# Attention and an expert layer in one kernel: the softmax of later batches moved to VectorE, and the order of work in the first two chunks changed

## The chip, the cores and the metric

The kernel runs on one core of one Trainium2 chip. The metric is device time in microseconds (us) of one execution. Each time given is the median of several runs, and one execution is also recorded by the hardware profiler. The core's engines are TensorE (PE, matrix products; PEld is its weight load), VectorE (DVE), ScalarE (ACT), GpSimd (POOL) and SyncE (SP, which issues the DMAs here). Each works through a queue of its own in order.

## The reference

Two stages, all in float32: attention with a window over 8 batches of 8 heads, 576 positions and 64 dimensions a head, then a two-layer block with an ELU.

```python
scores = q @ k.T / sqrt(64)              # per batch and head
rel = pos[:, None] - pos[None, :]
mask = (rel >= 0) & (rel < 32)                           # heads 0 to 3
mask = (rel >= 0) & (rel < 128) & (rel % 4 == 0)         # heads 4 to 7
attn = softmax(where(mask, scores, -1e9))
x = (attn @ v), heads side by side       # 4608 x 512
h = x @ w_in                             # 512 x 2048
g = where(h > 0, h, exp(min(h, 0)) - 1)
out = g @ w_out                          # 2048 x 512
```

The weights arrive as float64 bit patterns and are converted to float32 on the chip.

## The kernel before, in words

**Chunks.** The 4608 rows of x are taken in 9 chunks (c) of 512. For each chunk the 2048 hidden units are taken in 16 groups (f) of 128. Gemm1 of an f multiplies a 128-column slice of w_in with the chunk's x into a PSUM tile h; `elu` turns it into g; gemm2 adds g times w_out's rows into four PSUM banks (`o_ps`). Gemm2 of f is put two f behind gemm1 (LAG), so PE's order is gemm1(f), any attention work placed at f, gemm2(f - 2). PE keeps the order in which the program states its products. All products have one line in the profile, L82, and are told apart by their tiles: h is gemm1, o_ps gemm2, a_ps the attention's scores and outputs (in later chunks, tile h receives most of the attention's outputs too, from pt and vt).

**Two kinds of product.** A product is either one float32 matmul (recorded as two) or three float32r matmuls: each operand is split into a high part and a remainder, and high x high, high x low and low x high are added. For x the parts are xh and xl (`split_x`, L302 on ACT and L303 on DVE); for weights wh and wl (`split_w`, L131 on ACT and L132 on DVE); for g they are gh and gl (L340 on ACT, L341 on DVE). In chunk 0 both gemms use float32 for f < 12 (F0), since splits aren't ready; the float64 conversion (`magnitude` L102 on ACT, `convert` L110 to L115 on DVE) runs one weight pair after another through chunk 0. From f = 12 on all is float32r. The raw weights live in tiles r, their float32 form in tiles a, and the splits are written into whichever of these have come free.

**Elu.** For f < 12 of chunk 0: exp (L330) and a relu (L332) on ACT, one step on DVE (L334). Otherwise ACT first copies h from PSUM to SBUF (L328; one buffer), then exp (L330) on ACT, two steps on DVE (L336, L337), then gh on ACT and gl on DVE. In chunks 1 to 6 h has one PSUM bank (h0), as the other (h1) receives attention outputs; otherwise it has two.

**Attention.** The heads are handled in 4 pairs per batch. For a pair, 36 small products per head give the scores for 6 query blocks of 96 (windows of 64 keys each); DVE adds the mask (L253), takes the maximum (L254) and scales it (L255); ACT computes 12 exponentials with the sum accumulated (L259); sums are inverted (L181, L182) and multiplied in (L183, on DVE for batch 1, on POOL for later ones); six transposes on DVE (L265) write pt; PE multiplies with v, and ACT copies the outputs into x32 (L173, L176). Batch 0 is done before chunk 0 with other code (`first_attention`). Batch 1 is done during chunk 0 by the generator `batch_attention`, whose 8 steps are spread over f. Batches 2 to 7 are done during chunks 1 to 6, batch c + 1 during chunk c, in `piece`s: at a piece PE computes the outputs of the last pair and the scores of the next. The places of pieces are the f in `when`:

```python
when = () if c == 0 or c >= B - 1 else (0, 4, 7, 10, 12) if c == 1 else (2, 5, 9, 12)
```

So in chunk 1 the first piece only starts a softmax (at f = 0), and the last one starts batch 3.

**Order.** The program is laid out by a scheduler with a timing model: it fills each engine's queue by the order of statements and by when it believes operands are ready. `tc.issue_after(ins)` places the instructions of a block behind `ins` in that instruction's engine queue, with no wait of its own.

Of the kernel before, what the change touches and what calls it, by code (L numbers as in the profile page):

```python
# [46 lines left out]
def body(ctx: ExitStack, tc: tile.TileContext, q, k, v, masks, w_in, w_out, out):  # L47
# [69 lines left out]
    def split_w(k):  # L117

        if k >= K0:
            both = wst.tile([P, 2, 2, DM], F32R, name=f"r{k - K0}")  # L120
            h, l = both[:, 0, :, :], both[:, 1, :, :]
        else:
            l = wst.tile([P, 2, DM], F32R, name=f"a{k - 1}")
            slot = NF - K0 + k // 2
            if slot < NR:
                if k % 2 == 0:
                    split_w.room = wst.tile([P, 2, 2, DM], F32R, name=f"r{slot}")
                h = split_w.room[:, k % 2, :, :]
            else:
                h = wst.tile([P, 2, DM], F32R, name=f"a{K0 + k - 2 * (NR - NF + K0)}")  # L130
        nc.scalar.copy(out=h, in_=full2[k])  # L131
        nc.vector.tensor_tensor(out=l, in0=full2[k], in1=h.bitcast(F32), op=ALU.subtract)  # L132
        for t in range(2):
            wh[need[2 * k + t]], wl[need[2 * k + t]] = h[:, t, :], l[:, t, :]
# [108 lines left out]
    def probabilities(b, hp, loaded, s_ps):  # L243
# [11 lines left out]
        nc.vector.tensor_scalar(out=nmx, in0=nmx, scalar1=-0.125, scalar2=None, op0=ALU.mult)  # L255
        for u in range(2 * NU):
            if u == NU:
                yield
            nc.scalar.activation(out=sm[:, u, :], in_=sm[:, u, :], func=AF.Exp, bias=nmx[:, u:u + 1], scale=0.125, accum_out=sums[:, u:u + 1])  # L259
        normalise(nc.vector if b < 2 else nc.gpsimd, sm, sums, lambda ins: ins)  # L260
        tr = transposed()
        for c in range(GU):
            for r in range(2):
# [1 line left out]
                nc.vector.transpose(out=tr[ks, :, cs], in_=sm[cs, :, rs])  # L265
# [58 lines left out]
    def elu(h_ps, first):  # L324
        e = fp.tile([P, TC], F32, name="e", bufs=3)
        if not first:
            h = fp.tile([P, TC], F32, name="h", bufs=1)
            freed.append(nc.scalar.copy(out=h, in_=h_ps).ins)  # L328
# [1 line left out]
        nc.scalar.activation(out=e, in_=h_ps, func=AF.Exp)  # L330
# [6 lines left out]
        hidden.append(nc.vector.scalar_tensor_tensor(out=e, in0=h_ps, scalar=0.0, in1=e, op0=ALU.max, op1=ALU.add).ins)  # L337
# [20 lines left out]
    def batch_attention(b):  # L358

        x32[b] = xp.tile([P, NPAIR, S], F32, name="x32", bufs=2)  # L360

        old = None
        for hp in range(NPAIR):
            *_, new = probabilities(b, hp, loaded_pairs.pop((b, hp)), banks())
# [167 lines left out]
```

## Time and profile before

| what | value |
|---|---|
| median of 3 runs | 916.41 us (916.23 to 916.5) |
| profiled execution, its own time | 916.74 us |
| its span | 915.0 us |
| mean clock granted to PE | 0.991 |
| PE busy | 891.9 us (97%) |
| DVE busy | 553.6 us (61%) |
| ACT busy | 462.1 us (51%) |
| POOL busy | 46.3 us (5%) |
| DMA | 59.40 MB, mean 65 GB/s |

The span is from the first to the last recorded work. Chunk 0 takes roughly 30 to 140 us of it, chunk 1 140 to 249, and each of chunks 2 to 6 some 97 us. The share of an engine is an average over stages with different limits. In the timeline's rows, a bracket tells how long the engine stood idle just before, and what ended it. Matmuls overlap: rows can be longer than the distance to the next row's start, and it is this distance that counts.

### The profile page before, as it was taken

What the parts mean: (1) busy time and instruction counts of PE and PEld (TensorE: products, weight loads), DVE (VectorE), ACT (ScalarE), POOL (GpSimd) and SP (SyncE); (2) the same over time, 40 slices, a digit from 0 to 9 for tenths busy, and PEclk for the clock granted to TensorE, in tenths of its full rate; (3) what the DMA queues carried; (4) which work ended last, traced back from release to release, by engine and by line L of the source; (5) the groups of instructions that cost most, each with busy time, mean ns of one, the idle gap of its engine ahead of it and who ended that gap; (6) DMA issues with size and microseconds to landing.
All of it is one profiled execution on the core that took longest, in us unless ns stands there. A gap on an engine that the chain in (4) does not pass through costs nothing.

```text
span 915.0 us, 16120 instructions
## 1 busy us (share of the span) xinstructions
PE 891.9 (97%) x6536; PEld 698.0 (76%) x6536; DVE 553.6 (61%) x926; ACT 462.1 (51%) x1317; POOL 46.3 (5%) x36
## 2 busy tenths in 40 slices
PE   5999999998999999999999999999999999999998
PEld 4544458876888888888788888888888888888886
DVE  5999989676647565566565565656475433343332
ACT  4754595554555446545554555555545443344333
POOL 2000000100001000001000000000000000000000
PEclk8999999998999999999999999999999999999999
DMA  9963111111121112111121202111200010001001
GB/s 350 403 234 119 44 36 67 51 45 51 40 90 44 46 44 91 45 45 45 47 79 33 67 1 91 45 54 36 91 19 1 1 47 1 0 1 47 1 1 46
DMA packets 23803, 59.40 MB, mean 65 GB/s; under 512 B 2640, under 2 KB 2736, under 8 KB 23728
## 3 DMA queue, kind: packets, MB, share of 16 engines
q1 hardware_dynamic: 23728, 58.37, 18.7%
q8 instruction: 51, 0.84, 0.4%
q14 instruction: 24, 0.20, 0.1%
HBM read 48.92 MB, written 9.44 MB: 64 GB/s over the span
## 4 chain that ended last, share of the span: by engine, by line
PE 72%; DVE 14%; ACT 7%; DMA 4%; issue 3%; SPq 0%; ACTq 0%; DVEq 0%
PE h L82 35%; PE o_ps L82 33%; PE a_ps L82 3%; DVE pt L265 3%; DMA r<-w_out 2%; DVE e L337 2%; ACT sm L259 2%; DVE a L115 1%; DVE a L113 1%; ACT xh L302 1%; DVE a L132 1%; ACT r L131 1%; ACT h L328 1%; DMA r<-w_in 1%; DVE a L110 1%
## 5 line engine op out<-in xcount | busy, mean ns | idle before, releaser
L82 PE MATMUL o_ps<-a,gh 128*128 128x512 f32 x576 | 205.5, 426 | 0.0
L82 PE MATMUL o_ps<-r,gh 128*128 128x512 f32 x576 | 194.3, 396 | 0.3 <-ACT gh L340 0.3
L340 ACT CAST gh<-e 128x512 fp32r<-128x512 f32 x132 | 82.1, 622 | 217.7 <-DVE e L337 217.7
L82 PE MATMUL h<-xh,r 128*128 128x512 f32 x512 | 183.8, 393 | 0.8 <-ACT h L328 0.5
L82 PE MATMUL h<-xh,a 128*128 128x512 f32 x480 | 147.8, 389 | 0.0
L336 DVE TENSOR_SCALAR e<-e 128x512 f32<-128x512 f32 x132 | 56.2, 426 | 150.7 <-ACT e L330 148.3
L82 PE MATMUL o_ps<-r,gl 128*128 128x512 f32 x368 | 144.4, 392 | 1.5 <-DVE gl L341 1.5
L82 PE MATMUL h<-xl,r 128*128 128x512 f32 x368 | 143.3, 389 | 0.0
L328 ACT COPY h<-h 128x512 f32<-128x512 f32 x132 | 77.0, 583 | 128.3 <-PE h L82 128.3
L82 PEld LDWEIGHTS o_ps<-a,gh 128*128 128x128 f32 x576 | 107.3, 188 | 39.0 <-issue 19.6
L259 ACT ACTIVATE sm<-sm,nmx 96x64 f32<-96x64 f32 x336 | 112.4, 337 | 43.0 <-DVE nmx L255 43.0
L341 DVE TENSOR_TENSOR gl<-e,gh 128x512 fp32r<-128x512 f32 x132 | 91.3, 692 | 66.8 <-ACT gh L340 55.8
L82 PEld LDWEIGHTS o_ps<-r,gh 128*128 128x128 f32 x576 | 108.6, 190 | 24.3 <-ACT gh L340 0.5
L337 DVE SCALAR_TENSOR_TENSOR e<-h,e 128x512 f32<-128x512 f32 x132 | 119.0, 902 | 4.5
L82 PEld LDWEIGHTS h<-xh,r 128*128 128x128 f32 x512 | 96.3, 188 | 23.8 <-ACT h L328 3.2
L82 PEld LDWEIGHTS h<-xh,a 128*128 128x128 f32 x480 | 90.1, 188 | 18.8
L330 ACT ACTIVATE e<-h 128x512 f32<-128x512 f32 x144 | 90.4, 628 | 20.9 <-PE h L82 18.6
L265 DVE STREAM_TRANSPOSE pt<-sm 32x384 f32<-32x384 f32 x168 | 95.4, 568 | 1.9
L82 PEld LDWEIGHTS o_ps<-r,gl 128*128 128x128 f32 x368 | 69.6, 189 | 16.6 <-DVE gl L341 1.9
L82 PEld LDWEIGHTS h<-xl,r 128*128 128x128 f32 x368 | 69.2, 188 | 14.9 <-issue 0.7
L183 POOL TENSOR_TENSOR sm<-sm,sums 96x768 f32<-96x768 f32 x24 | 40.3, 1680 | 644.8 <-ACT e L330 644.8
L181 DVE TENSOR_SCALAR sums<-sums 96x12 f32<-96x12 f32 x32 | 6.0, 189 | 108.9 <-ACT sm L259 108.7
(92 smaller groups left out, 824.2 us busy)
## 6 DMA issues: line engine op xcount, KB each, us to landing
vt<-v SPq DMA_DIRECT2D x30, 384.0 KB, 3.4
kt<-k SPq DMA_DIRECT2D x30, 304.0 KB, 4.7
qt<-q SPq DMA_DIRECT2D x30, 288.0 KB, 4.3
r<-w_in SPq DMA_DIRECT2D x16, 512.0 KB, 8.1
r<-w_out SPq DMA_DIRECT2D x16, 512.0 KB, 8.3
out<-o SPq DMA_DIRECT2D x32, 256.0 KB, 2.2
out<-xl SPq DMA_DIRECT2D x4, 256.0 KB, 2.1
r<-v SPq DMA_DIRECT2D x2, 384.0 KB, 8.6
```

The lines of the kernel that those rows point to most:

```text
L82: inorder(nc.tensor.matmul(*args, **kw))
L110: keep(nc.vector.tensor_scalar(out=a, in0=a, scalar1=TINY, scalar2=None, op0=ALU.max))
L113: keep(nc.vector.scalar_tensor_tensor(out=au, in0=hi, scalar=0xC0000000, in1=au, op0=ALU.bitwise_and, op1=ALU.bitwise_or))
L183: return keep(eng.tensor_tensor(out=sm, in0=sm, in1=sums.unsqueeze(2).broadcast_to([QB, 2 * NU, 2 * G]), op=ALU.mult))
L259: nc.scalar.activation(out=sm[:, u, :], in_=sm[:, u, :], func=AF.Exp, bias=nmx[:, u:u + 1], scale=0.125, accum_out=sums[:, u:u + 1])
L265: nc.vector.transpose(out=tr[ks, :, cs], in_=sm[cs, :, rs])
L328: freed.append(nc.scalar.copy(out=h, in_=h_ps).ins)
L330: nc.scalar.activation(out=e, in_=h_ps, func=AF.Exp)
L336: nc.vector.tensor_scalar(out=e, in0=e, scalar1=1.0, scalar2=-1.0, op0=ALU.min, op1=ALU.add)
L337: hidden.append(nc.vector.scalar_tensor_tensor(out=e, in0=h_ps, scalar=0.0, in1=e, op0=ALU.max, op1=ALU.add).ins)
L340: nc.scalar.copy(out=gh, in_=e)
L341: nc.vector.tensor_tensor(out=gl, in0=e, in1=gh.bitcast(F32), op=ALU.subtract)
```

## The change

- **Float32r in chunk 0.** F0 = 12 becomes two numbers: gemm1 uses float32r from f = 9 (F1), gemm2 from f = 14 (F2). `split_w` takes parts of a weight pair (only the w_in half for pairs 8 to 14 in chunk 0), and `space` hands out room for the parts. `split_x(0)` comes at f = 6 instead of 8. In chunk 1 the remaining parts are split: pairs 0 to 7 whole, 8 to 14 by half.
- **Elu.** Through chunk 0, and in chunks 7 and 8, h isn't copied to SBUF. All of chunk 0 uses ACT's relu.
- **Softmax of batches 2 to 7.** DVE subtracts the maximum, ACT computes one exponential over the pair's whole tile (96 x 768), DVE sums it, and DVE (not POOL) multiplies. Batch 1 keeps the old form, on DVE throughout. `probabilities` is divided into `exponentials` (E) and `probabilities` (X), and nothing is held back to the next f in a piece.
- **Places.** Batch 1's steps are written out, one entry per f: scores and exponentials (E) at f = 1, 3, 7, 11; X at 2, 4, 8, 12; outputs (O) at 5, 9, 14, 15, where before the outputs were at 5, 9, 13, 14. The pieces of chunk 1 move from (0, 4, 7, 10, 12) to (0, 3, 6, 9, 12).
- **Order.** Several `issue_after` anchors move with it.

The diff, cut to its core:

```diff
-F0 = 12
-K0 = F0 - 1
+F1 = 9
+F2 = 14
...
+    spaces = [[f"r{i}", 4] for i in range(NR)] + [["a-1", 2]]
+    taken = {}
+    def space(n):
+        s = next(s for s in spaces if s[1] >= n)
+        if s[0] not in taken:
+            taken[s[0]] = wst.tile([P, s[1], DM], F32R, name=s[0]), s[1]
+        room, all_of = taken[s[0]]
+        o = all_of - s[1]
+        s[1] -= n
+        return room[:, o:o + n, :]
+    def split_w(k, t0, t1):
+        h, l = space(t1 - t0), space(t1 - t0)
+        w = full2[k][:, t0:t1, :]
+        nc.scalar.copy(out=h, in_=w)
+        nc.vector.tensor_tensor(out=l, in0=w, in1=h.bitcast(F32), op=ALU.subtract)
+        for t in range(t0, t1):
+            wh[need[2 * k + t]], wl[need[2 * k + t]] = h[:, t - t0, :], l[:, t - t0, :]
+        if all(wh[need[2 * k + t]] is not None for t in range(2)):
+            spaces.append([f"a{k}", 2])
...
-        nc.vector.tensor_scalar(out=nmx, in0=nmx, scalar1=-0.125, scalar2=None, op0=ALU.mult)
-        for u in range(2 * NU):
-            if u == NU:
-                yield
-            nc.scalar.activation(out=sm[:, u, :], in_=sm[:, u, :], func=AF.Exp, bias=nmx[:, u:u + 1], scale=0.125, accum_out=sums[:, u:u + 1])
-        normalise(nc.vector if b < 2 else nc.gpsimd, sm, sums, lambda ins: ins)
+        if b == 1:
+            nc.vector.tensor_scalar(out=nmx, in0=nmx, scalar1=-0.125, scalar2=None, op0=ALU.mult)
+            for u in range(2 * NU):
+                nc.scalar.activation(out=sm[:, u, :], in_=sm[:, u, :], func=AF.Exp, bias=nmx[:, u:u + 1], scale=0.125, accum_out=sums[:, u:u + 1])
+        else:
+            nc.vector.tensor_tensor(out=sm, in0=sm, in1=nmx.unsqueeze(2).broadcast_to([QB, 2 * NU, 2 * G]), op=ALU.subtract)
+            nc.scalar.activation(out=sm, in_=sm, func=AF.Exp, scale=0.125)
+            nc.vector.tensor_reduce(out=sums, in_=sm, op=ALU.add, axis=mybir.AxisListType.X)
+        return b, hp, vt, sm, sums
+    def probabilities(b, hp, vt, sm, sums):
+        normalise(nc.vector, sm, sums, lambda ins: ins)
         tr = transposed()
         for c in range(GU):
             for r in range(2):
                 ks, cs, rs = slice((c + r) * G, (c + r + 1) * G), slice(c * G, (c + 1) * G), slice(r * G, (r + 1) * G)
-                nc.vector.transpose(out=tr[ks, :, cs], in_=sm[cs, :, rs])
+                last_transpose[b] = nc.vector.transpose(out=tr[ks, :, cs], in_=sm[cs, :, rs]).ins
+        return b, hp, vt, tr
...
-        if c == 0 and f < F0:
+        if c == 0 and f < F1:
...
-    def elu(h_ps, first):
+    def elu(h_ps, c, f):
         e = fp.tile([P, TC], F32, name="e", bufs=3)
-        if not first:
+        if 0 < c < B - 1:
             h = fp.tile([P, TC], F32, name="h", bufs=1)
-            freed.append(nc.scalar.copy(out=h, in_=h_ps).ins)
+            nc.scalar.copy(out=h, in_=h_ps)
             h_ps = h
         nc.scalar.activation(out=e, in_=h_ps, func=AF.Exp)
-        if first:
+        if c == 0:
             below.append(nc.scalar.activation(out=e, in_=e, func=AF.Relu, scale=-1.0, bias=1.0).ins)
-            g = fp.tile([P, TC], F32, name="gh", bufs=3)
-            hidden.append(nc.vector.scalar_tensor_tensor(out=g, in0=h_ps, scalar=0.0, in1=e, op0=ALU.max, op1=ALU.subtract).ins)
-            return g, None
-        nc.vector.tensor_scalar(out=e, in0=e, scalar1=1.0, scalar2=-1.0, op0=ALU.min, op1=ALU.add)
-        hidden.append(nc.vector.scalar_tensor_tensor(out=e, in0=h_ps, scalar=0.0, in1=e, op0=ALU.max, op1=ALU.add).ins)
+            if f < F2:
+                g = fp.tile([P, TC], F32, name="gh", bufs=3)
+                hidden.append(nc.vector.scalar_tensor_tensor(out=g, in0=h_ps, scalar=0.0, in1=e, op0=ALU.max, op1=ALU.subtract).ins)
+                return g, None
+            hidden.append(nc.vector.scalar_tensor_tensor(out=e, in0=h_ps, scalar=0.0, in1=e, op0=ALU.max, op1=ALU.subtract).ins)
+        else:
+            nc.vector.tensor_scalar(out=e, in0=e, scalar1=1.0, scalar2=-1.0, op0=ALU.min, op1=ALU.add)
+            nc.vector.scalar_tensor_tensor(out=e, in0=h_ps, scalar=0.0, in1=e, op0=ALU.max, op1=ALU.add)
...
+    def second_attention():
+        x32[1] = xp.tile([P, NPAIR, S], F32, name="x32", bufs=2)
+        state = [None] * NPAIR
+        for step in " E0 X0 E1 X1 O0  E2 X2 O1  E3 X3  O2 O3".split(" "):
+            if step:
+                what, hp = step[0], int(step[1])
+                if what == "E":
+                    state[hp] = exponentials(1, hp, loaded.pop((1, hp)), banks())
+                    load_next(1, hp)
+                elif what == "X":
+                    state[hp] = probabilities(*state[hp])
+                else:
+                    b, _, vt, tr = state[hp]
+                    outputs(b, hp, [(a, i * NA, (i + 1) * NA) for i, a in enumerate(banks())], vt, tr)
             yield
-            if old is not None:
-                outputs(*old[:2], [(a, i * NA, (i + 1) * NA) for i, a in enumerate(banks())], *old[2:])
-                yield
-            old = new
-        outputs(*old[:2], [(a, i * NA, (i + 1) * NA) for i, a in enumerate(banks())], *old[2:])
...
-            with tc.issue_after(hidden[F0 - 4]), tc.issue_after(below[F0 - 4]):
-                split_x(c)
+            with tc.issue_after(hidden[-4]), tc.issue_after(below[-4]):
+                last_x = split_x(c)
         elif c > 1:
             split_x(c)
-        att = batch_attention(c + 1) if c == 0 else iter(())
-        when = () if c == 0 or c >= B - 1 else (0, 4, 7, 10, 12) if c == 1 else (2, 5, 9, 12)
-        emitted = 0
+        when = () if c == 0 or c >= B - 1 else (0, 3, 6, 9, 12) if c == 1 else (2, 5, 9, 12)
...
-            if c == 0 and f == F0 - 4:
+            if c == 0 and f == F1 - 3:
                 with tc.issue_after(hidden[-1]), tc.issue_after(below[-1]):
                     split_x(0)
-            if c == 0 and K0 <= f + 2 < NF:
+            if c == 0 and F1 <= f + 2 <= NF:
                 with tc.issue_after(hidden[-1]):
-                    split_w(f + 2)
-            while c == 1 and split < min(K0, f + 2):
-                with tc.issue_after(hidden[NF - 4 if split < 2 else NF - 1]):
-                    split_w(split)
+                    split_w(f + 1, 0, 2 if f >= F2 else 1)
+            while c == 1 and split < min(NF, f + 2):
+                left = [t for t in range(2) if wh[need[2 * split + t]] is None]
+                with tc.issue_after(last_transpose[1] if split < 2 else last_x):
+                    if left:
+                        split_w(split, left[0], left[-1] + 1)
                 split += 1
-            pend.append((c, f, elu(gemm1(c, f), c == 0 and f < F0)))
-            if steps is not None and (c, f) != (1, 1):
-                with tc.issue_after(freed[-1]):
-                    current, steps = next(steps), None
+            pend.append((c, f, elu(gemm1(c, f), c, f)))
+            if c == 0:
+                with tc.issue_after(hidden[-1] if f > 1 else last_step[NPAIR - 1]):
+                    next(att)
             if f in when:
                 n = (c + 1) * NPAIR + when.index(f) + NPAIR + 1 - len(when)
-                current, steps = None, piece(current, divmod(n, NPAIR) if n < B * NPAIR else None)
-            while emitted < (f + 1) * STEPS // (NF - 1):
-                emitted += 1
-                if c == 0 and emitted <= 2:
-                    with tc.issue_after(last_step[NPAIR - 1]):
-                        next(att, None)
-                else:
-                    next(att, None)
+                current = piece(current, divmod(n, NPAIR) if n < B * NPAIR else None)
```

More of the change, by code (lines that the diff above doesn't have):

```diff
@@ L115, in convert @@
         return keep(nc.vector.scalar_tensor_tensor(out=au, in0=lo, scalar=29, in1=au, op0=ALU.logical_shift_right, op1=ALU.bitwise_or))
[L117 to L121, printed above, removed]
-        else:
[L123 to L134, printed above, removed]
+    spaces = [[f"r{i}", 4] for i in range(NR)] + [["a-1", 2]]
[17 more added lines that the diff above has]
+            spaces.append([f"a{k}", 2])
     x32 = {}
     last_step = [None] * NPAIR
+    last_transpose = [None] * B
     count = [0]
@@ L241, in first_attention, with exponentials @@
         yield outputs(0, hp, [(a_ps[:, i, :], i * NA, (i + 1) * NA) for i in range(NU // NA)], vt, tr, inorder)
-    def probabilities(b, hp, loaded, s_ps):
+    def exponentials(b, hp, loaded, s_ps):
         dil = hp >= NPAIR // 2
@@ L264, in probabilities, with load_next @@
                 ks, cs, rs = slice((c + r) * G, (c + r + 1) * G), slice(c * G, (c + 1) * G), slice(r * G, (r + 1) * G)
-                nc.vector.transpose(out=tr[ks, :, cs], in_=sm[cs, :, rs])
+                last_transpose[b] = nc.vector.transpose(out=tr[ks, :, cs], in_=sm[cs, :, rs]).ins
+        return b, hp, vt, tr
+    def load_next(b, hp):
         nxt = b * NPAIR + hp + 1
         if nxt < B * NPAIR:
-            loaded_pairs[divmod(nxt, NPAIR)] = load_pair(*divmod(nxt, NPAIR))
-        yield b, hp, vt, tr
+            loaded[divmod(nxt, NPAIR)] = load_pair(*divmod(nxt, NPAIR))
     def piece(old, new):
@@ L281, in piece @@
             return None
-        steps = probabilities(*new, loaded_pairs.pop(new), a)
-        next(steps)
-        return steps
+        p = probabilities(*exponentials(*new, loaded.pop(new), a))
+        load_next(*new)
+        return p
     xh, xl = [None] * NC, [None] * NC
     hidden, below = [], []
-    freed = []
     def split_x(c):
@@ L302, in split_x @@
                 nc.scalar.copy(out=xh[hp][:, u], in_=src)
-                nc.vector.tensor_tensor(out=xl[hp][:, u], in0=src, in1=xh[hp][:, u].bitcast(F32), op=ALU.subtract)
+                last = nc.vector.tensor_tensor(out=xl[hp][:, u], in0=src, in1=xh[hp][:, u].bitcast(F32), op=ALU.subtract)
                 t0 += n
+        return last.ins
     def product1(c, f):
@@ L356, in store @@
             nc.sync.dma_start(out=out[c * TC + t * P:c * TC + (t + 1) * P, :], in_=o)
[L358 to L364, printed above, removed]
-            yield
-            if old is not None:
-                outputs(*old[:2], [(a, i * NA, (i + 1) * NA) for i, a in enumerate(banks())], *old[2:])
-                yield
-            old = new
-        outputs(*old[:2], [(a, i * NA, (i + 1) * NA) for i, a in enumerate(banks())], *old[2:])
-        yield
-    STEPS = 2 * NPAIR
-    loaded_pairs = {}
+    def second_attention():
[12 more added lines that the diff above has]
+                    outputs(b, hp, [(a, i * NA, (i + 1) * NA) for i, a in enumerate(banks())], vt, tr)
+            yield
+    loaded = {}
     rooms = [room(0, hp) for hp in range(NPAIR)]
@@ L408, in body @@
     ps_a = ctx.enter_context(tc.tile_pool(name="ps_a", bufs=1, space=bass.MemoryType.PSUM))
-    loaded_pairs[1, 0] = load_pair(1, 0)
+    loaded[1, 0] = load_pair(1, 0)
     for j in range(NR - NE, NR + 2):
@@ L412, in body @@
     split = 0
-    current = steps = None
+    current = None
     pend = []
@@ L424, in flush @@
                 store(c, o_of.pop(c))
+    att = second_attention()
     for c in range(NCH):
         if c == 1:
-            with tc.issue_after(hidden[F0 - 4]), tc.issue_after(below[F0 - 4]):
-                split_x(c)
+            with tc.issue_after(hidden[-4]), tc.issue_after(below[-4]):
+                last_x = split_x(c)
         elif c > 1:
             split_x(c)
-        att = batch_attention(c + 1) if c == 0 else iter(())
-        when = () if c == 0 or c >= B - 1 else (0, 4, 7, 10, 12) if c == 1 else (2, 5, 9, 12)
-        emitted = 0
+        when = () if c == 0 or c >= B - 1 else (0, 3, 6, 9, 12) if c == 1 else (2, 5, 9, 12)
         for f in range(NF):
```

1 line of the change is left out of this document (removed).

## The prediction

> **What bounds the kernel now.** I read the page first: busy shares, then the chain that ended last.
>
> ```profile
> span 915.0 us, 16120 instructions
> PE 891.9 (97%) x6536; PEld 698.0 (76%) x6536; DVE 553.6 (61%) x926; ACT 462.1 (51%) x1317; POOL 46.3 (5%) x36
> ...
> PE 72%; DVE 14%; ACT 7%; DMA 4%; issue 3%; SPq 0%; ACTq 0%; DVEq 0%
> ```
>
> TensorE (PE) works for 97% of the span, so what counts is PE's own work and the places where it stands still. The chain in order of time gives the price of the work, and the table of stretches shows where PE isn't dense (columns: length, busy time of PE, weight load, DVE, ACT, POOL, then the granted clock).
>
> ```profile
> 194.50 2.72 PE h L82 x12
> ```
> ```profile
> 40.00:138.00 98.00, 95.95 (x535) 48.77 (x534) 94.30 (x133) 62.53 (x163) 0.00 (x0) 0.98 0.36 124
> 249.00:345.70 96.70, 96.48 (x769) 78.91 (x769) 58.95 (x105) 50.60 (x165) 6.72 (x4) 1.00 0.17 53
> 134.00:138.00 4.00, 3.86 (x11) 3.00 (x12) 2.94 (x5) 3.01 (x7) 0.00 (x0) 0.61 0.04 13
> 225.00:232.00 7.00, 7.00 (x107) 5.96 (x108) 3.73 (x7) 2.29 (x9) 0.00 (x0) 0.61 0.45 139
> ```
>
> Twelve float32r products (one gemm of one f) take 2.72 us. A later chunk (249 to 345.7) is dense at clock 1.00. Chunk 0 (40 to 138) is not, and there VectorE (DVE) too is full: 94.3 of 98 us. In 134 to 138 and 225 to 232 the clock is 0.61. The timeline of PE shows what happened just before both (start, length, then the idle time and what ended it).
>
> ```profile
> 98.70 3.60 PE L82 MATMUL h<-x,a 128*128 128x512 f32 x8
> ...
> 105.57 3.60 PE L82 MATMUL h<-x,a 128*128 128x512 f32 x8
> ...
> 113.13 0.80 PE L82 MATMUL h<-xh,r 128*128 128x512 f32 x1
> ...
> 119.32 0.79 PE L82 MATMUL h<-xh,r 128*128 128x512 f32 x1
> ...
> 126.83 0.79 PE L82 MATMUL h<-xh,r 128*128 128x512 f32 x1
> ...
> 130.36 1.21 PE L82 MATMUL a_ps<-pt,vt 128*64 128x96 f32 x24 [0.21 <-ACT x L173]
> 131.92 0.73 PE L82 MATMUL o_ps<-r,gh 128*128 128x512 f32 x2 [0.35 <-ACT gh L340]
> 134.14 0.50 PE L82 MATMUL o_ps<-r,gl 128*128 128x512 f32 x1 [1.49 <-DVE gl L341]
> ...
> 137.99 0.55 PE L82 MATMUL h<-xh,r 128*128 128x512 f32 x1
> ...
> 140.90 0.61 PE L82 MATMUL o_ps<-r,gh 128*128 128x512 f32 x2
> ...
> 190.57 0.97 PE L82 MATMUL a_ps<-kt,qt 64*32 64x64 f32 x72 [1.15 <-ACT x L176]
> ...
> 208.03 0.39 PE L82 MATMUL a_ps<-pt,vt 128*64 128x96 f32 x4
> ...
> 213.03 0.39 PE L82 MATMUL h<-xh,a 128*128 128x512 f32 x1
> ...
> 224.94 0.59 PE L82 MATMUL a_ps<-pt,vt 128*64 128x96 f32 x4 [3.59 <-issue]
> ...
> 232.25 0.39 PE L82 MATMUL h<-xh,r 128*128 128x512 f32 x1
> ```
>
> Three stalls, each priced with the slow matmuls behind it:
>
> **Stall A, f = 14 of chunk 0.** Gemm1 of f 14 starts at 126.83, that of f 15 at 137.99: 11.16 us. Between them lie two gemms of 2.72 and 24 small output matmuls (1.21), so 6.65 would do: 4.5 lost. The next gemm (137.99 to 140.90) takes 2.91 instead of 2.72. Together 4.7, though the idle times in brackets sum to only 2.05; the rest is the clock of 0.61. What PE waits for is the first gl of the kernel, that of f 12.
>
> **Stall B, f = 12 of chunk 1.** 3.59 us idle, put down to "issue". The piece and the gemm behind it then take 7.31 (224.94 to 232.25), against 5.00 for the same work at f = 10 (208.03 to 213.03). So 3.59 + 2.31 = 5.9. The timelines of DVE and POOL name the cause:
>
> ```profile
> 133.40 0.69 DVE L341 TENSOR_TENSOR gl<-e,gh 128x512 fp32r<-128x512 f32 x1
> ...
> 219.60 1.84 DVE L337 SCALAR_TENSOR_TENSOR e<-h,e 128x512 f32<-128x512 f32 x1
> 221.37 3.47 DVE L265 STREAM_TRANSPOSE pt<-sm 32x384 f32<-32x384 f32 x6
> ...
> 225.94 0.69 DVE L337 SCALAR_TENSOR_TENSOR e<-h,e 128x512 f32<-128x512 f32 x1
> ```
> ```profile
> 219.22 1.68 POOL L183 TENSOR_TENSOR sm<-sm,sums 96x768 f32<-96x768 f32 x1 [17.01 <-ACT e L330]
> ```
>
> The transposes that this piece's outputs read end at 224.84; PE goes on at 224.94. Pieces 7, 10 and 12 of chunk 1 leave the last softmax only two f. Scores of f = 10 end at about 210.3 (213.03 less one gemm), so the softmax needs 14.6 us, and two f of PE are 4 x 2.72 = 10.9.
>
> **Stall C, f = 7 of chunk 1**: 1.15 us, PE behind ACT's copy of outputs, no slow clock after it: 1.1.
>
> **The change part by part.** The grouped lines give the durations (busy, mean ns).
>
> ```profile
> L259 ACT ACTIVATE sm<-sm,nmx 96x64 f32<-96x64 f32 x336 | 112.4, 337 | 43.0 <-DVE nmx L255 43.0
> L253 DVE TENSOR_TENSOR sm<-a_ps,masks_sb 96x384 f32<-96x384 f32 x56 | 28.3, 545 | 2.1 <-PE a_ps L82 2.1
> L214 DVE TENSOR_TENSOR r<-b,nmx 96x768 f32<-96x768 f32 x2 | 1.9, 953 | 0.1
> L216 ACT ACTIVATE r<-r 96x768 f32<-96x768 f32 x3 | 2.5, 843 | 4.6 <-DVE r L214 4.6
> L218 DVE TENSOR_REDUCE sums<-r 96x12 f32<-96x768 f32 x3 | 2.8, 927 | 2.4 <-ACT r L216 2.4
> L183 DVE TENSOR_TENSOR sm<-sm,sums 96x768 f32<-96x768 f32 x5 | 4.8, 950 | 0.1
> L265 DVE STREAM_TRANSPOSE pt<-sm 32x384 f32<-32x384 f32 x168 | 95.4, 568 | 1.9
> L328 ACT COPY h<-h 128x512 f32<-128x512 f32 x132 | 77.0, 583 | 128.3 <-PE h L82 128.3
> L330 ACT ACTIVATE e<-h 128x512 f32<-128x512 f32 x144 | 90.4, 628 | 20.9 <-PE h L82 18.6
> L341 DVE TENSOR_TENSOR gl<-e,gh 128x512 fp32r<-128x512 f32 x132 | 91.3, 692 | 66.8 <-ACT gh L340 55.8 <-PE o_ps L82 10.3
> L132 DVE TENSOR_TENSOR a<-a,r 128x1024 fp32r<-128x1024 f32 x5 | 6.1, 1215 | 0.0
> L173 ACT COPY x<-a_ps 128x288 f32<-128x288 f32 x4 | 1.4, 393 | 0.0
> ```
>
> *Products of chunk 0.* Two float32 gemms take 6.87 (98.70 to 105.57), one of each kind 6.19 (113.13 to 119.32), two of float32r 5.44. Gemm1 of f 9, 10, 11 turns to float32r: 3 x 0.68 = 2.04 gained. Gemm2 of f 12 and 13 turns back to float32: 2 x 0.75 = 1.50 lost. **Net -0.5.**
>
> *The first gl.* With F2 = 14 the first gl is that of f 14, and PE needs it only after the first gemm1 of chunk 1, two f later than now. DVE's work before that shrinks: elu of f 12 and 13 keeps one DVE step of three (0.69 left; gone are the gl of 0.69 and a shorter one), and f 14 and 15 lose the shorter one. Weight splits stay equal: 5 x 1.22 before; after, one of 1.22 and seven halves, each about 0.69 (an estimate from the 128x512 subtraction of gl), 6.05. The splits of f 9 to 11 and of x come earlier in a DVE queue that is full, and push the conversions of weights by some 3 us; I take that as free, since it is cover that ends at the gemm1 that reads the converted weight. What is late next is the last transposes of batch 1: they stay one f ahead of O3, which is itself one f later. **Stall A goes: -4.7.**
>
> *Pieces at 0, 3, 6, 9, 12.* Each softmax of chunk 1 now has three f, 6 x 2.72 = 16.3 us, where 14.6 was enough. **Stall B goes: -5.9**, even with the old softmax.
>
> *New softmax.* Per pair ACT drops 12 exponentials of 0.337 (4.0 us, without their accumulator reads) for one of 0.843. DVE gains a subtraction (0.953), a sum (0.927) and the multiplication (0.950, POOL's until now), and drops a tiny scaling. Part of this comes back: while POOL multiplies (219.22 to 220.90), DVE's step of 0.69 takes 1.84, so 1.15 per pair returns. The chain from scores to transposes is 2 x 0.545 + 0.93 + 0.953 + 0.843 + 0.927 + 0.950 + 6 x 0.568 = 9.1 us, with one elu in between some 11 instead of 14.6. In the later chunks, where PE is busy for 96.48 of 96.70 us, this is worth nothing, as it lies beside PE. In chunk 1 DVE comes sooner to the elu that ACT's cast, and behind it the copy of stall C, waited for: **-1.1**, between 0 and 1.15.
>
> *Cover in the later chunks.* There h has one PSUM bank and one copy in SBUF. Count from the end of gemm1 of f with a piece behind it: scores are done at 2.2 (the piece is 5.00 less a gemm), the softmax with elu's steps between at about 12.4, then elu of f + 1 (1.1 on DVE) at 13.5, and only then ACT may copy h of f + 2 (0.58): 14.1. PE wants the bank after 2.2 + 5 x 2.72 = 15.8. Cover 1.7 us; each us beyond it would be paid at 25 pieces.
>
> *Chunk 7 and 8, and the end of chunk 0, without the copy of h.* ACT saves 0.58 per f; PE alternates two banks there, so the bank is freed by DVE's step a whole f ahead of its use. 0.
>
> *Border of chunk 0 and 1.* O3 now comes after gemm1 of f 15. PE then has O3 (1.2) and a float32 gemm2 (3.43) before gemm1 of chunk 1 needs xh, 4.6 us where it was one gemm of 2.9. ACT must fit in two copies of x (0.39 each) that were earlier before. Chunk 1 also has 15 weight splits in place of 11, eight of 1.22, and its first piece must be through by f = 3 instead of 4. No row shows this order. Bounds: 0, as PE waits for no xh now, and 2.4, two splits of 1.22 in the wrong place. I take **+1.0**, nearer to the present zero.
>
> *Queues.* SP's loads of the next pair are issued when the exponentials are, ahead of the transposes; the v tile still waits for the outputs two pairs back, now one f later, and is read three f later. 0. POOL has nothing left after the start.
>
> **Sum.** -0.5 - 4.7 - 5.9 - 1.1 + 1.0 = -11.2. The profiled execution took 916.74 (915.0 of span and 1.7 around it), 0.33 above the median of the runs, 916.41. So 905.5 there, and **905.2** as a median.
>
> **The rivals.**
>
> *The first softmax of chunk 1 is late at f = 3.* DVE then has the splits, elu and 9.1 us of softmax. For: DVE was full up to 138. Against: 16.3 us against 11 and two or three splits. PE would stand as it did in stall B: 905.2 + 5.9 = 911.1.
>
> *The border stalls.* DVE's backlog only moves from f 14 to the splits of x. Stall A's price returns: 909.9. Against: the longer window.
>
> *The slow clock isn't the stalls'.* Then only the bare waits return in A: 2.05 instead of 4.7, or 907.9. The trace speaks against it: 0.61 stands right behind a gap each time, 1.00 elsewhere. [...]
>
> *Slower: the burst on DVE.* The six transposes now follow the multiplication with nothing between, so elu of f + 1 stands behind 9 us of softmax. If the burst runs over the cover of 1.7, PE waits for its bank at each of some 25 pieces. At 1 us over that is 25: 930. It decides from 11.2 / 25 = 0.45 us over, that is a burst 2.1 us longer than I count. For: DVE takes its queue in order. Against: DVE is busy for 58.95 of 96.70 us there, and the 1.15 under POOL goes.
>
> *The pieces do not get through sooner*, since the order on DVE puts other work ahead: both stalls stay, 916.
>
> **How the numbers follow.** Likeliest 0.62 (own range 903 to 907.5: the +1.0 between 0 and 2.4, C kept or gone, about 1 us for prices read off single rows), first softmax 0.12, border 0.10, clock 0.04, burst 0.10, nothing 0.02. The range 903 to 911.5 holds the first four cases but for their edges, 8 in 10. Faster 0.88, same 0.02, slower 0.10; the bound is 0.2%, 1.8 us, about what a measurement of this kernel can tell from no change.
>
> **What would show it.** Right: no PE idle of over 1 us between 120 and 235 us of the span, the clock at 1.00 after chunk 0's start, gemm1 of chunk 1 starting about 5 us sooner, POOL silent after 25 us, PE's later chunks still about 96.7. DVE's step L337 should never take 1.84. Wrong: a bracket of several us at the outputs of f = 3 of chunk 1, at its first gemm1, or short ones behind ACT's copy of h at every piece; a later chunk longer than 96.8 refutes the cover that I count.

## The result, and the profile after

The changed kernel takes 907.67 us (906.96 to 908.62), the kernel before 916.32 beside it: 0.9907 of its time, with a 95% interval of 0.989 to 0.9924. That is 8.65 us less. 905.2 was forecast, with a range of 903 to 911.5; the likeliest case had 903 to 907.5 for itself. The profiled execution took 906.96. Its page begins so, again busy shares and the chain:

```profile
span 905.2 us, 15526 instructions
PE 884.9 (98%) x6540; PEld 695.9 (77%) x6540; DVE 587.5 (65%) x975; ACT 369.4 (41%) x738; POOL 6.0 (1%) x12
...
PE 86%; DVE 8%; issue 2%; ACT 2%; DMA 1%; POOL 0%; SPq 0%; DVEq 0%; ACTq 0%
```

The work moved as the diff says: ACT 93 us less, DVE 34 more, POOL silent after the start. PE's share of the chain rose from 72 to 86%. The steps of the new softmax cost what the nearest rows said (grouped lines of the changed kernel: busy, mean ns, idle before):

```profile
L190 DVE TENSOR_TENSOR sm<-sm,sums 96x768 f32<-96x768 f32 x29 | 27.6, 953 | 0.8
L268 DVE TENSOR_TENSOR sm<-sm,nmx 96x768 f32<-96x768 f32 x24 | 22.9, 954 | 0.8
L270 DVE TENSOR_REDUCE sums<-sm 96x12 f32<-96x768 f32 x24 | 22.8, 949 | 8.0 <-ACT sm L269 8.0
L269 ACT ACTIVATE sm<-sm 96x768 f32<-96x768 f32 x24 | 20.3, 848 | 51.8 <-DVE sm L268 51.8
```

Stretches of the changed kernel (columns as in the prediction): chunk 0, and chunk 2 from its first product to that of chunk 3.

```profile
40.00:138.00 98.00, 97.18 (x557) 52.30 (x558) 94.41 (x138) 58.83 (x163) 0.00 (x0) 1.00 0.36 123
241.50:337.70 96.20, 96.20 (x769) 79.08 (x768) 65.48 (x113) 38.55 (x73) 0.00 (x0) 1.00 0.17 54
```

In chunk 0 the clock is 1.00, and in chunk 2 PE has no idle time at all. PE's timeline shows what is left between 120 and 242 us:

```profile
126.01 0.50 PE L82 MATMUL h<-xh,r 128*128 128x512 f32 x1 [0.82 <-DVE gh L351]
...
144.03 0.97 PE L82 MATMUL a_ps<-kt,qt 64*32 64x64 f32 x72
...
164.46 0.39 PE L82 MATMUL a_ps<-pt,vt 128*64 128x96 f32 x4 [2.90 <-issue]
...
220.28 0.39 PE L82 MATMUL a_ps<-pt,vt 128*64 128x96 f32 x4
```

Stalls A, B and C are gone (220.28 is the piece at f = 12, without a bracket). Two new ones stand in their place: 0.82 us at gemm1 of f 14 of chunk 0, and 2.90 us at the outputs of f = 3 of chunk 1, the place that the first rival named. DVE's timeline tells why (L136 is the weight split, L280 the transposes):

```profile
149.28 1.21 DVE L136 TENSOR_TENSOR a<-a,a 128x1024 fp32r<-128x1024 f32 x1
...
160.28 0.68 DVE L136 TENSOR_TENSOR a<-a,a 128x512 fp32r<-128x512 f32 x1
160.88 3.47 DVE L280 STREAM_TRANSPOSE pt<-sm 32x384 f32<-32x384 f32 x6
164.39 0.69 DVE L356 SCALAR_TENSOR_TENSOR e<-h,e 128x512 f32<-128x512 f32 x1
```

The transposes end at 164.35, PE goes on at 164.46. PE ended the scores of this softmax at 145.00 (144.03 + 0.97), so the softmax took 19.4 us, where three f of PE are 16.3. Between DVE's first step on the scores (148.35) and these transposes lie six weight splits, the first and the last of them shown; five more stand ahead of that step.

For all kernels of this study, the distance from one chunk's first gemm1 to the next's on PE's timeline divides the span. "Start" is gemm1 of f 2 in chunk 0; it varies by 1.6 us between executions, though the programs hardly differ up to there.

```
kernel (profiled execution)         start  chunk 0  chunk 1  chunks 2-6  rest   span
before                              38.79   104.83   105.26    482.67   183.45  915.0
changed                             39.97   100.80   100.76    480.23   183.44  905.2
e1 old places                       38.91   100.84   100.79    480.23   183.43  904.2
e2 old softmax                      38.51   100.80   103.87    479.67   183.45  906.3
e3 multiplication on POOL           39.81   100.84   103.05    479.68   183.42  906.8
e4 splits behind first softmax      38.86   100.82    99.39    479.67   183.46  902.2
e5 before, last piece at 13         39.26   103.28   100.77    486.63   183.46  913.4
e6 before, nothing held back        39.39   104.83   101.85    480.23   183.40  909.7
e7 F1 = F2 = 12                     39.13   102.96   105.88    480.23   183.40  911.6
e8 F1 = 12, F2 = 14                 38.58   103.21   105.03    480.24   183.44  910.5
e9 e8 with e4's order               38.97   103.26    99.80    480.23   183.44  905.7
e10 e4, one exponential in pair 3   40.12    99.70    99.86    480.23   183.39  903.3
e11 last outputs at 13, 14          39.12   101.87   103.86    480.23   183.42  908.5
e12 changed, again                  39.52   100.80   100.75    480.23   183.40  904.7
```

Chunk 0 gained 4.03, chunk 1 4.50, chunks 2 to 6 together 2.44; the start lost 1.18.

### The profile page after: what moved, and what is told of

Read it like the earlier page. It is cut to its first block, busy times and chain, and to the rows that moved or that the text cites. A ratio compares the mean times of both kernels' runs of the same rounds, so it can differ in the third digit from the quotient of the medians.

```text
span 905.2 us, 15526 instructions
## 1 busy us (share of the span) xinstructions
PE 884.9 (98%) x6540; PEld 695.9 (77%) x6540; DVE 587.5 (65%) x975; ACT 369.4 (41%) x738; POOL 6.0 (1%) x12
## 4 chain that ended last, share of the span: by engine, by line
PE 86%; DVE 8%; issue 2%; ACT 2%; DMA 1%; POOL 0%; SPq 0%; DVEq 0%; ACTq 0%
PE h L82 42%; PE o_ps L82 41%; PE a_ps L82 3%; DVE a L115 1%; DVE a L113 1%; DVE a L110 1%; DVE pt L280 1%; DVE gh L351 1%; DVE a L112 1%; ACT pt L245 1%; DMA kt<-k 1%; ACT sm L266 0%; DVE sm L260 0%; PE a L82 0%; DVE sm L190 0%
## 5 line engine op out<-in xcount | busy, mean ns | idle before, releaser
L82 PE MATMUL o_ps<-a,gh 128*128 128x512 f32 x816 | 270.6, 421 | 0.0
L82 PE MATMUL h<-xh,r 128*128 128x512 f32 x792 | 264.9, 393 | 0.8 <-DVE gh L351 0.8
L82 PEld LDWEIGHTS h<-xh,r 128*128 128x128 f32 x792 | 148.7, 188 | 34.1 <-DVE gh L351 1.9
L82 PE MATMUL o_ps<-a,gl 128*128 128x512 f32 x352 | 137.1, 389 | 0.0
L82 PE MATMUL o_ps<-r,gh 128*128 128x512 f32 x304 | 97.1, 392 | 0.0
L280 DVE STREAM_TRANSPOSE pt<-sm 32x384 f32<-32x384 f32 x168 | 95.4, 568 | 1.9
L82 PE MATMUL h<-xh,a 128*128 128x512 f32 x256 | 84.0, 389 | 0.0
L82 PEld LDWEIGHTS o_ps<-a,gl 128*128 128x128 f32 x352 | 66.1, 188 | 14.2
L82 PEld LDWEIGHTS o_ps<-r,gh 128*128 128x128 f32 x304 | 56.5, 188 | 12.1
L82 PE MATMUL o_ps<-r,gl 128*128 128x512 f32 x168 | 65.5, 390 | 0.0
L82 PE MATMUL h<-xl,a 128*128 128x512 f32 x128 | 49.8, 389 | 0.0
```

The source lines that it names most:

```text
L82: inorder(nc.tensor.matmul(*args, **kw))
L280: last_transpose[b] = nc.vector.transpose(out=tr[ks, :, cs], in_=sm[cs, :, rs]).ins
```

## The experiments

**e1: are the new places needed?**

```diff
-(0, 3, 6, 9, 12) if c == 1
+(0, 4, 7, 10, 12) if c == 1
```

> The changed kernel (907.7) with the pieces of chunk 1 at (0, 4, 7, 10, 12) again. Theory L (the new softmax is short enough for two f): in chunk 2 of the changed kernel it takes 10.95 us from the end of the scores to the end of the transposes, and two f of TensorE are 10.9. Then the piece at f = 12 stalls by 0.5 us at most, the stall of 2.9 us at f = 3 goes, as that piece has a whole f more, and the time is 904.8 (904 to 905.6). Theory S (as the prediction had it, the spacing alone took stall B away, whatever the softmax): the stall at f = 12 returns with its slow clock, 3 to 6 us, and the time is 908 to 911.

906.58 us, 0.9901 (0.9885 to 0.9916): the same as the changed kernel. PE of this kernel, at f = 4 and at the piece of f = 12, and DVE ahead of the first:

```profile
165.24 0.50 PE L82 MATMUL h<-xh,r 128*128 128x512 f32 x1 [1.99 <-ACT h L344]
...
220.46 0.97 PE L82 MATMUL a_ps<-kt,qt 64*32 64x64 f32 x72 [0.67 <-ACT x L180]
```
```profile
159.85 3.48 DVE L280 STREAM_TRANSPOSE pt<-sm 32x384 f32<-32x384 f32 x6
163.36 0.69 DVE L356 SCALAR_TENSOR_TENSOR e<-h,e 128x512 f32<-128x512 f32 x1
```

Theory L's main claim holds: with two f behind it, the new softmax no longer makes the outputs of f = 12 wait. Its sum (904.8) failed, since the stall of f = 3 only changed its form: elu's second step stands behind the transposes until 163.36, ACT can copy h only after it, and PE waits 1.99 us for the bank. That is the burst of the slower rival, at one place. The places add nothing to the new softmax.

**e2: the old softmax in the changed program.**

```diff
-        if b == 1:
+        if True:
...
-        normalise(nc.vector, sm, sums, lambda ins: ins)
+        normalise(nc.vector if b < 2 else nc.gpsimd, sm, sums, lambda ins: ins)
```

> The changed kernel with the old softmax for all batches (12 exponentials a pair on ScalarE, the multiplication on GpSimd), places and products as changed. Theory L: the softmax's length counts in two places. The first one of chunk 1 gets 3.7 us longer, so the stall at f = 3 grows from 2.9 to some 6.6 us, perhaps with a slow clock behind it (2.3); chunks 2 to 6 go back from 96.2 to 96.8 us each (2.4 in all). Time 913.8 to 916. Rival: the stall at f = 3 is set by the weight splits and not by the softmax's length; it stays at about 2.9, and only the later chunks pay: 910.1.

909.53 us, 0.9935 (0.9921 to 0.9948); neither theory. PE's stalls in chunk 1, and the stretch of chunk 2:

```profile
157.78 1.22 PE L82 MATMUL o_ps<-r,gh 128*128 128x512 f32 x2 [2.42 <-ACT o L374]
164.30 0.39 PE L82 MATMUL a_ps<-pt,vt 128*64 128x96 f32 x4
...
176.40 0.50 PE L82 MATMUL h<-xh,a 128*128 128x512 f32 x1 [1.60 <-ACT h L344]
```
```profile
243.20:339.30 96.10, 96.10 (x770) 79.11 (x769) 57.76 (x105) 51.46 (x165) 5.89 (x4) 1.00 0.17 54
```

The outputs of f = 3 (164.30) wait for nothing: the transposes ahead of them end 23.5 us after the chunk's first gemm1, as in the changed kernel (23.6), and PE comes later. So with the splits ahead of it this softmax is not made later by its old form. What the old form costs in chunk 1, 3.1 us, comes from ACT, whose 4 us of exponentials (12 of 0.335) hold up the copies of o and h (waits of 2.42 and 1.60), and from slow matmuls behind the wait of 2.42: up to 160.5 they start 0.43 us apart, where 0.23 is the distance before it. And chunk 2 is as short as with the new one. So neither the softmax's form nor POOL gave the later chunks their 0.5 us each; another part of the change did (e6).

**e3: only the multiplication back on POOL.**

```diff
-        normalise(nc.vector, sm, sums, lambda ins: ins)
+        normalise(nc.vector if b < 2 else nc.gpsimd, sm, sums, lambda ins: ins)
```

> The changed kernel with only the multiplication of the later batches back on GpSimd (1.68 us in place of 0.95 on VectorE), one exponential a pair as changed. Theory L (the length of the softmax counts): 0.7 us more at the stall of f = 3, the borders of chunks 2 to 6 stay free: 908.4 (907.7 to 909.2). Rival P (what freed the borders is that VectorE's step of 0.69 us no longer takes 1.84 beside GpSimd): chunks 2 to 6 go back to 96.8 us: 910.8.

908.88 us, 0.9926 (0.9913 to 0.9939): the time is theory L's. PE at f = 3, and the stretch behind it beside chunk 2:

```profile
165.44 0.59 PE L82 MATMUL a_ps<-pt,vt 128*64 128x96 f32 x4 [3.98 <-issue]
```
```profile
165.40:169.00 3.60, 3.56 (x97) 3.28 (x98) 3.04 (x6) 1.93 (x4) 0.00 (x0) 0.60 0.10 21
```

The stall grows by 1.1 us instead of 0.7, and now the clock falls to 0.60 behind it: chunk 1 takes 2.3 us more. Chunks 2 to 6 take 479.68, so rival P falls; why they are 0.55 shorter than in the changed kernel is open, and it hides part of the loss.

**e4: the weight splits behind the first softmax.**

```diff
-                with tc.issue_after(last_transpose[1] if split < 2 else last_x):
+                with tc.issue_after(last_transpose[1] if split < 2 else last_x if split < 4 else first_transpose):
...
                 current = piece(...)
+                if (c, f) == (1, 0):
+                    first_transpose = last_transpose[2]
```

> The changed kernel, with the weight splits of chunk 1 from the fifth pair on queued on VectorE behind the transposes of that chunk's first softmax. Theory W (weight splits that fill VectorE's queue make that softmax late): in the changed kernel six of them lie between its scores and its transposes (4.1 us), and more ahead of its start. Without them the stall of 2.9 us at f = 3 goes: 904.8 (904 to 905.8). Rival: the softmax with the steps of elu alone needs more than the three f: a stall of 1.5 us or more stays, 906.3 to 908; or the splits are then late for the products that read them and the stall moves to a later f: 907 or more.

904.5 us, 0.9878 (0.9865 to 0.9891). DVE, then PE from f = 3 on:

```profile
152.62 3.47 DVE L280 STREAM_TRANSPOSE pt<-sm 32x384 f32<-32x384 f32 x6
```
```profile
161.00 0.39 PE L82 MATMUL a_ps<-pt,vt 128*64 128x96 f32 x4
...
181.82 0.97 PE L82 MATMUL a_ps<-kt,qt 64*32 64x64 f32 x72 [1.03 <-ACT x L183]
```

The transposes end at 156.1 instead of 164.4, five us before PE comes for them. Theory W is shown: the splits made that softmax late. But a wait of 1.03 us appears at the next piece, and chunk 1 gains only 1.37 of the 2.9. That the time is theory W's 904.8 nearly to the figure is partly luck: chunks 2 to 6 gained 0.56 that was not forecast, and the start came 1.1 earlier in the profiled execution.

**e5: the kernel before with one piece moved.**

```diff
-(0, 4, 7, 10, 12) if c == 1
+(0, 4, 7, 10, 13) if c == 1
```

> The kernel before with one piece moved: chunk 1's pieces at (0, 4, 7, 10, 13), so that the last one has three f behind it. Theory S (stall B is the old softmax against two f): the softmax of 14.6 us fits into 16.3, the idle time of 3.6 us and the slow clock behind it go, stall C at f = 7 stays: 916.1 - 5.9 = 910.2 (909.4 to 911.2). Rival: the idle time put down to issue is something in TensorE's own supply of instructions, and comes back at this place or another: 915 to 917.

913.82 us, 0.998 (0.9971 to 0.9989). PE at the moved piece and at the border to chunk 2, and DVE ahead of the border:

```profile
226.78 0.39 PE L82 MATMUL a_ps<-pt,vt 128*64 128x96 f32 x4
...
243.31 0.51 PE L82 MATMUL h<-xh,r 128*128 128x512 f32 x1 [0.43 <-ACT h L328]
245.12 0.50 PE L82 MATMUL h<-xl,r 128*128 128x512 f32 x1 [1.30 <-DVE xl L303]
```
```profile
240.20 3.47 DVE L265 STREAM_TRANSPOSE pt<-sm 32x384 f32<-32x384 f32 x6
```

Stall B is gone with the spacing alone; chunk 1 takes 100.77 instead of 105.26. But the last piece's softmax now falls on the border: its transposes end at 243.67, and the xl that chunk 2 needs stand behind them. Chunks 2 to 6 lose 3.96, of which 3.5 in chunk 2. Theory S has the cause right, its 910.2 not.

**e6: the kernel before, nothing held back.**

```diff
-        steps = probabilities(*new, loaded_pairs.pop(new), a)
-        next(steps)
-        return steps
+        *_, whole = probabilities(*new, loaded_pairs.pop(new), a)
+        return whole
```

> The kernel before, with nothing of a softmax held back to the next f: the 12 exponentials of a later pair are issued in one go. Theory H (holding half of them back cost the later chunks their 0.6 us each, as the run with the old softmax suggests, in which chunks 2 to 6 took 96.1 us): chunks 2 to 6 go from 96.8 to 96.1, 3 us in all; at f = 12 of chunk 1 the softmax takes 13.4 us instead of 14.6, so stall B shrinks by 1.2. Time 916.1 - 4.2 = 911.9 (911 to 913.5). Rival: the 0.6 us came from chunks 0 and 1 leaving the queues in another state, or from the places of the loads, and stay: 915 to 917.

911.52 us, 0.9958 (0.9945 to 0.9971), as theory H said; stall B shrank by 1.28 us, against 1.2, and the slow clock behind it went as well (1.00 from 224.8 to 228.0, against 0.61 from 225 to 232 in the kernel before). Chunk 2, and stall B:

```profile
246.07:342.30 96.23, 96.23 (x770) 79.08 (x768) 57.78 (x105) 51.68 (x165) 5.89 (x4) 1.00 0.17 54
```
```profile
224.85 0.39 PE L82 MATMUL a_ps<-pt,vt 128*64 128x96 f32 x4 [2.31 <-issue]
```

Chunks 2 to 6 take 480.23, to the hundredth what they take in the changed kernel: all of their gain is that a softmax is no longer split over two f. In the kernel before, PE lost it at the borders, as at that to chunk 3, where two gemms take 5.93 us (342.66 to 348.59) instead of 5.44:

```profile
342.66 0.62 PE L82 MATMUL o_ps<-r,gh 128*128 128x512 f32 x2
...
348.59 0.62 PE L82 MATMUL o_ps<-r,gh 128*128 128x512 f32 x2
```

ACT at the border to chunk 3 shows how, in the kernel before and in the changed one at the border to chunk 2:

```profile
342.70 0.62 ACT L340 CAST gh<-e 128x512 fp32r<-128x512 f32 x1 [3.41 <-DVE e L337]
343.22 1.94 ACT L302 CAST xh<-x 128x192 fp32r<-128x192 f32 x6
```
```profile
237.03 0.62 ACT L359 CAST gh<-e 128x512 fp32r<-128x512 f32 x1 [1.22 <-DVE e L356]
238.33 1.95 ACT L317 CAST xh<-x 128x128 fp32r<-128x128 f32 x6 [0.68 <-PE h L82]
```

Before, ACT stood 3.41 us for an elu that was late on DVE behind the softmax, and the casts of x came after it. After, ACT is idle there and waits for PE.

**e7: the old products.**

```diff
-F1 = 9
-F2 = 14
+F1 = 12
+F2 = 12
```

> The changed kernel with the float32r products of both gemms from f = 12 on, as before (F1 = F2 = 12). Theory A (stall A went because the first gl is needed two f later): it is needed at f = 14 again, with the same full VectorE ahead of it; the stall and its slow clock come back, 3.5 to 4.7 us, and the products themselves cost 0.5: 911.5 (910.5 to 913). Rival: it went because elu is cheaper through all of chunk 0 and the outputs of batch 1 come later; then only the products count: 908.2.

912.13 us, 0.9966 (0.9954 to 0.9978). The time is theory A's, the places aren't. PE:

```profile
128.23 0.50 PE L82 MATMUL h<-xh,r 128*128 128x512 f32 x1 [1.86 <-DVE e L353]
...
157.95 0.80 PE L82 MATMUL h<-xh,r 128*128 128x512 f32 x1 [2.62 <-ACT h L344]
...
170.88 0.39 PE L82 MATMUL a_ps<-pt,vt 128*64 128x96 f32 x4 [1.57 <-issue]
```

No product waits for gl. Chunk 0 loses 2.16 us, by the products and a longer wait for the bank at f = 14; chunk 1 loses 5.1, to waits for ACT's copy of h and for the transposes and to slow matmuls behind the wait of 2.62, which start 0.43 us apart instead of 0.23. Why gl was late before, and isn't here, is seen at the exponential of f = 12, first in the kernel before, then in this one, with this one's gl:

```profile
129.40 0.63 ACT L330 ACTIVATE e<-h 128x512 f32<-128x512 f32 x1
```
```profile
124.45 0.58 ACT L346 ACTIVATE e<-h 128x512 f32<-128x512 f32 x1
```
```profile
131.11 0.68 DVE L360 TENSOR_TENSOR gl<-e,gh 128x512 fp32r<-128x512 f32 x1
```

Before, ACT cast five weight splits (124.66 to 129.50) between its copy of h and this exponential, and DVE took two splits ahead of gl, which it reached at 133.40. Here the exponential comes ahead of the casts, and gl is done over 1 us before PE takes it.

**e8: only gemm1 back (F1 = 12).**

> The changed kernel with gemm1 in float32 up to f = 11 again (F1 = 12), gemm2 as changed (F2 = 14). Theory: three gemms cost 0.68 more each, and the stall of 0.82 us at f = 14 (with its slow matmuls 1.1) stays: 909.7. Rival: the earlier splits of weights push VectorE's and ScalarE's work of batch 1 and make that stall; with them later it goes, and TensorE takes longer to reach f = 14 as well: 908.6.

913.27 us, 0.9975 (0.9966 to 0.9985): above both. PE:

```profile
127.03 0.50 PE L82 MATMUL h<-xh,r 128*128 128x512 f32 x1 [1.19 <-DVE gh L351]
...
168.31 0.59 PE L82 MATMUL a_ps<-pt,vt 128*64 128x96 f32 x4 [3.94 <-issue]
```

Chunk 0 takes 2.41 more: 2.04 for three gemms, as forecast, and 0.37 by the wait at f = 14, which is still there and longer, so the earlier splits aren't its cause. Chunk 1 takes 4.27 more: three half splits have moved into it.

**e9: e8's products with e4's order.** The edits of both.

> Gemm1 in float32 up to f = 11 (F1 = 12, F2 = 14) together with the weight splits of chunk 1 queued behind the first softmax's transposes. With F1 = 12 alone chunk 1 took 105.0 us instead of 100.8, beside the 2.4 us that chunk 0 took longer. Theory W (those 4.3 us are weight splits that moved from chunk 0 into chunk 1 and fill VectorE's queue ahead of its first softmax): with the order changed chunk 1 is back at 99.4 to 100.5 us, and the time is 913.3 less some 5 us, 908.3 (907 to 909.5). Rival: the loss in chunk 1 comes from chunk 0 ending with a backlog on VectorE and ScalarE; the order of the splits matters little: 911 or more.

907.42 us, 0.9907 (0.9891 to 0.9922). Chunk 1 is back at 99.80, and the outputs of f = 3 come without a bracket:

```profile
162.95 0.39 PE L82 MATMUL a_ps<-pt,vt 128*64 128x96 f32 x4
```

So e8's loss in chunk 1 was the splits, as theory W has it, and not a backlog out of chunk 0 (103.26, unchanged).

**e10: e4, and one exponential in the last pair of batch 1.**

```diff
-        if b == 1:
+        if b == 1 and hp < NPAIR - 1:
```

> The changed kernel with the splits of chunk 1 behind the first softmax (904.5), and with the last pair of batch 1 in the new form of softmax too (subtraction and sum on VectorE, one exponential). Theory E (the wait of 0.82 us at f = 14 of chunk 0 is elu's exponential of f = 12, queued on ScalarE behind the 24 steps of that pair's exponentials, 4 us): with one step of 0.85 it goes, with its slow matmuls 1.1 us: 903.4 (902.8 to 904.3). Rival: VectorE, busy for 94 of 98 us in chunk 0, pays 1.7 us more there, and the border to chunk 1 stalls instead: 904.5 to 906.5.

904.37 us, 0.9873 (0.9855 to 0.9892). ACT in the changed kernel, from the first of the pair's 12 exponentials (24 steps, as each has a read of its sum) to elu of f = 12, then in this one, then this one's PE at f = 14:

```profile
118.67 0.35 ACT L266 ACTIVATE sm<-sm,nmx 96x64 f32<-96x64 f32 x1 [3.83 <-DVE nmx L264]
...
122.67 0.57 ACT L346 ACTIVATE e<-h 128x512 f32<-128x512 f32 x1
...
124.61 0.63 ACT L348 ACTIVATE e<-e 128x512 f32<-128x512 f32 x1
```
```profile
115.78 0.60 ACT L346 ACTIVATE e<-h 128x512 f32<-128x512 f32 x1 [0.80 <-PE h L82]
```
```profile
124.78 0.79 PE L82 MATMUL h<-xh,r 128*128 128x512 f32 x1
```

Chunk 0 falls by 1.12, and no wait is left at f = 14, so theory E is shown in the main: elu stood behind that pair's softmax on ACT. The scheduler also put elu's exponential ahead of the pair's single one here (115.78 against 119.59), so whether fewer steps or the other order did it is not separated. But chunk 1 takes 0.47 more than in e4, with waits of 0.66 and 1.06, and chunks 2 to 6 take 0.56 more, so the total stays where e4 had it. e4 and e10 are the fastest versions measured.

**e11: the last outputs earlier.**

```diff
-E3 X3  O2 O3"
+E3 X3 O2 O3 "
```

> The changed kernel with the last two outputs of batch 1 at f = 13 and 14 again, as before (all else as changed). Theory: the transposes of the last pair end at 131.3 us in the changed kernel, and TensorE would reach these outputs at about 129; it waits 2.4 us, with a slow clock perhaps 1.5 more: 910 to 911.6. Rival: the last outputs' place is free, since something else (the wait at f = 14, the border) absorbs it: 907 to 908.3.

910.18 us, 0.994 (0.992 to 0.9961). PE in chunk 0 and in chunk 1:

```profile
130.54 1.21 PE L82 MATMUL a_ps<-pt,vt 128*64 128x96 f32 x24 [2.11 <-issue]
...
165.43 0.59 PE L82 MATMUL a_ps<-pt,vt 128*64 128x96 f32 x4 [3.68 <-issue]
```

The wait for the transposes is 2.11, with no slow matmuls behind it: the 24 outputs take 1.14 us to the next product, as in the changed kernel. The rest of the loss is chunk 1, whose stall at f = 3 grows to 3.68 and does bring them: the 20 outputs right behind it take 1.78 us instead of 0.95. Chunk 0 takes 1.07 more and chunk 1 3.10: the sum was right, three quarters of it at another place.

**e12: the changed kernel beside these.**

> The changed kernel itself, beside the others of this call on one chip: 907.7 (907 to 908.4), with the stall of 2.9 us at f = 3 of chunk 1 and that of 0.8 us at f = 14 of chunk 0.

906.85 us, 0.9904 (0.9886 to 0.9923), with the same two stalls and the same chunks to 0.02 us; only the start differs.

## Why the prediction was right, point by point

- **Products of chunk 0 (-0.5).** Three gemm1 in float32 cost 2.04 us by e8, as forecast; the other 0.37 there is the wait at f = 14. Right as a cost on PE, but the larger effect was missed: each split that chunk 0 takes over is one less in chunk 1 (4.27 us by e8 and e9).
- **Stall A (-4.7).** It is gone, and chunk 0 with its border gained 4.03 where -0.5 - 4.7 + 1.0 = -4.2 was forecast. The reason given, the later first gl, isn't what the runs show: with F2 = 12 no product waits for gl either (e7), as elu's exponential comes 5 us sooner, ahead of the weight splits on ACT. Whether the missing copy of h or the new order of the splits brought it forward was not separated. With the outputs at their old place 1.07 us of the gain is lost (e11). Stall A's price was also partly chance: e5, the same program up to there with a wait of 1.5 for gl by its page as well, took 103.28 where the kernel before and e6 took 104.83.
- **Stall B (-5.9) and C (-1.1).** Both gone. The cause of B, a softmax against two f, is shown twice: by spacing (e5) and by a shorter softmax (e1). The prediction named the spacing alone; either does it, but spacing alone moved the burst to the border.
- **The first softmax (rival, 0.12).** It came true at half its price: 2.90 us without a slow clock behind it (1.00 from 164.4 to 168.0), not 5.9. The step that failed is "16.3 us against 11 and two or three splits": eleven splits stood ahead of the transposes, six of them behind DVE's first step on the scores, and the softmax took 19.4 us. Chunk 1 therefore gained 4.50 and not 7.0. Of the signs that the prediction named, "no PE idle of over 1 us" failed here, and its sign of being wrong, a bracket of several us at the outputs of f = 3, stands in the trace.
- **The border (+1.0).** No bracket stands there. What took about that much was 1.35 us at f = 14, where PE wants the bank that elu of f 12 still holds; that the +1.0 fits is luck. The prediction had put chunk 0 without the copy of h at 0. Before, the copy freed the bank at 124.75, right behind the pair's 12 exponentials on ACT; now it is held until DVE's step ends at 125.96, behind the exponentials, elu's own, two casts of splits and the relu (e10).
- **Later chunks (0).** -2.44, from a part that the prediction listed only among the diff's edits: nothing is held back any more (e6). It was mis-sized because "96.48 of 96.70 busy" was read as dense: the borders' two gemms took 5.93 us instead of 5.44 (e6) while PE counted as busy.
- **The burst (rival, 0.10).** At no piece of the later chunks does PE wait, so the cover held there. In chunk 1, with splits in the queue, the mechanism shows (1.99 us in e1).
- **The sum.** Without the start, which came 1.18 later by no doing of the change, the profiled executions differ by 10.97 us, against 11.2; the terms' errors (+2.5 in chunk 1, -2.4 in chunks 2 to 6) cancelled, which is luck. The medians differ by 8.65: the profiled execution was the fastest of its four, that of before 0.42 above its median. 907.67 lies just outside the 903 to 907.5 of the likeliest case, and inside the whole range thanks to the room left for the rivals.

## What to carry to other kernels

When work moves to another engine, look for the place where that engine's queue is fullest, not at its mean load: here VectorE had room in every later chunk (65.5 us busy of 96.2 in chunk 2), and the one softmax that met the weight splits gave back 2.9 us. A wait that vanishes at one place is worth what the next late thing leaves of it: moving one piece removed 4.5 us of chunk 1 and cost 4.0 in the chunks behind it. And a stretch that a profile calls busy can still hide time: compare the distance between starts with the densest stretch of the same work.
